# Two pieces for the first heads, four units per row of 256-column products, and a shorter halved tail in a float32 attention and feed-forward kernel

## The chip, the cores and the metric

One core of a Trainium2 chip runs one kernel. The metric is device time of an execution in microseconds (us); less is better. Three runs of the kernel before took 1053.59, 1054.35 and 1054.69 us, so its median is 1054.35 us.

## What is computed

Attention with a sigmoid in place of the softmax, then two feed-forward blocks on the 1792 tokens (4 batches of 448), all in float32:

```python
scores = scale * np.matmul(q, k.transpose(0, 1, 3, 2)) - np.log(S)
attn = 1.0 / (1.0 + np.exp(-scores))
x = np.matmul(attn, v)                       # 4 x 12 heads, 448 x 64, regrouped to 1792 x 768
h = x @ w_in;  r = np.maximum(h, 0.0);  g = s * (r * r) + b;   x = g @ w_out
h = x @ w_in2; g = np.maximum(h, 0.0) + alpha * np.minimum(h, 0.0);  y = g @ w_out2
```

Widths are 768 (model) and 2048 (inner). The feed-forward weights arrive as 64-bit floats.

## The kernel before, in words

**Attention.** 24 pairs of heads give 84 steps. Step u issues the score products of its 128 keys (`emit_qk`, four matmuls of 64x448), the sigmoid on ACT (`emit_sig`), and, two steps behind, the products with V (`emit_av`). Ahead of it, `NWARM` = 6 rounds of four matmuls on a tile of zeros (L345) keep the engine at work while the first DMA is under way. `load_kq(0)` fetches the first pair's q and k with two DMAs of SP's queue, 576 columns and then 320.

**Feed-forward.** The tokens go in groups: 768 tokens, 512 and 512 for the first block, and the same for the second. For each group there are 34 *units*: 16 of the first product (kind "in", six blocks of 128 rows each) and 18 of the second (kind "out": six outputs, each in three cuts of 6, 5 and 5 blocks). I number the units of a group 0 to 33. A float32 operand is split into a high part `hi` and a rest `lo`, and three products (hi by hi, hi by lo, lo by hi) are summed. For a group of 768 tokens, 512 of the columns take these three products (L411 to L413, 512 columns each, called *longs* here together with L416), and the other 256 tokens take one matmul of 512 columns that covers hi by hi and hi by lo at once (L416) and one of only 256 columns for lo by hi (`short`, L402, called *shorts*). A unit of six blocks thus has 24 longs and 6 shorts. Even units do the shorts last and odd units first, so that the shorts of two units stand in one row.

**The other engines.** The loop over `steps` sets the order on every engine. In step n it issues: the products of unit n; `evac` of unit n-1; `split_unit(n + 2)`; `fetch(n + 5)`. `split_unit` makes a unit's weights: `hi` by a cast on ACT (L99), `lo` by a subtraction on DVE (L102); without it no matmul of that unit that uses `lo` can run. `evac` of an "in" unit copies the sums on ACT (L437), then adds, squares and scales on DVE (L439, L447, L454; in the second block L461 and L465), casts on ACT (L210) and subtracts on DVE (L217): that makes `g`, the operand of the "out" units. `fetch` loads weights, or, where they still are 64-bit (for "out" units in the first use), converts them (`convert`: L141 on ACT, L147, L152 and L155 on DVE). Every engine works through its own list in order. PE's tiles of sums are four, the split weights have four buffers.

**The last unit** (L494) runs as two halves of 256 columns over its five blocks; the copy (L501) and the store of the first half overlap the second half; the add (L503) and a second store end the kernel.

Of the kernel before, what the change touches and what calls it, by code (L numbers as in the profile page):

```python
# [12 lines left out]
ALU = mybir.AluOpType  # L13
# [3 lines left out]
P = 128  # L17
OUT_CUTS = [(0, 6), (6, 11), (11, 16)]

PASSES = [(0, 0), (0, 1), (0, 2), (1, 0), (1, 1), (1, 2)]  # L20
N5 = 512
NWARM = 6

# [13 lines left out]
def tile_kernel(  # L37
# [13 lines left out]
    nc = tc.nc  # L51
    B, NPR, _, SKQ = kq.shape
    S = SKQ // 2
    NCH = vt.shape[4]
    D = vt.shape[5]
    NK = NPR
    DM = NK * P
    NFC = w_in1.shape[0]
# [5 lines left out]
    TG = N5 + REST  # L64
    TOK = [TG, N5, N5]
    TOK0 = [0, TG, TG + N5]
    NCUT = len(OUT_CUTS)
    PER = NFC + NK * NCUT
# [22 lines left out]
    def t_tile(name):  # L91
        return tp.tile([P, TG], F32, tag="t", name=name)
# [27 lines left out]
    uses = [m * PER + j for m, _ in PASSES for j in range(PER)]  # L120
    r64, w32, wraw, whl = {}, {}, {}, {}
# [76 lines left out]
    x, x_dram, xr = {}, {}, {}  # L198
# [41 lines left out]
    kqt, vtt, sct, sgt, avt = {}, {}, {}, {}, {}  # L240
# [7 lines left out]
    def buffer(what, cols):  # L248
        first, n = place[what]
        t = ga[first + taken[what] % n]  # L250
        taken[what] += 1
        return t[:, WMAX : WMAX + cols]

    def tiles(u):

        q, c = order[u]
        if c == NCH - 1:
            return [(h, q + h, c * P) for h in range(2)]
        return [(h, q, c * P + h * D) for h in range(2)]

    def load_kq(q):
        if q < B * NPR:
            bb, pr = divmod(q, NPR)
            kqt[q] = buffer("kq", SKQ)

            cuts = [0, S + P, SKQ] if q == 0 else [0, SKQ]
            for a, e in zip(cuts, cuts[1:]):
                nc.sync.dma_start(out=kqt[q][:, a:e], in_=kq[bb, pr, :, a:e])

    def load_v(q):  # L270
        if q < B * NPR:
# [3 lines left out]

    def emit_qk(u):
        sc = acc_tile("sc") if u != 2 else av_tile("sc")
        for h, q, k0 in tiles(u):
            for j in range(2):
                rows = slice(j * D, (j + 1) * D)  # L280
                nc.tensor.matmul(  # L281
                    sc[h * D : (h + 1) * D, j, :S],
                    kqt[q][rows, S + k0 : S + k0 + D],
                    kqt[q][rows, :S],
                    start=True, stop=True,
                )
        sct[u] = sc

    def emit_sig(u):
# [50 lines left out]
    wp = av_tile("wp")  # L340
    for _ in range(NWARM):
        for h in range(2):
            for j in range(2):
                rows = slice(j * D, (j + 1) * D)
                nc.tensor.matmul(  # L345
                    wp[h * D : (h + 1) * D, j, :P], idle[rows, :D], idle[rows],
                    start=True, stop=True,
# [16 lines left out]
    for u in range(NU + 2):  # L364
# [7 lines left out]
        if u >= 2:  # L372
            q, c = order[u - 2]
# [5 lines left out]
        if u in conv_step:  # L379
            k = conv_step[u]  # L380
            w = ga[k][:, :WMAX]
# [11 lines left out]

    g, hp, op_ = {}, {}, {}

    def products(dst, p, terms, first, last, short_first):

        n = len(terms) - 1

        def short(start, stop):  # L400
            for k, (hi, lo, mv) in enumerate(terms):
                nc.tensor.matmul(  # L402
                    dst[:, N5:TG], lo, mv[:, 2 * N5 : N5 + TG],
                    start=start and k == 0, stop=stop and k == n, skip_group_check=True,
                )

        if p == 0 and short_first:
            short(first, False)
        for k, (hi, lo, mv) in enumerate(terms):
            end = last and k == n  # L410
            nc.tensor.matmul(dst[:, :N5], hi, mv[:, N5 : 2 * N5], start=first and k == 0, stop=False)  # L411
            nc.tensor.matmul(dst[:, :N5], hi, mv[:, :N5], start=False, stop=False)  # L412
            nc.tensor.matmul(dst[:, :N5], lo, mv[:, N5 : 2 * N5], start=False, stop=end)  # L413
        if p == 0:
            for k, (hi, lo, mv) in enumerate(terms):
                nc.tensor.matmul(  # L416
                    dst[:, N5 : 2 * N5], hi, mv[:, 2 * N5 :],
                    start=first and not short_first and k == 0,
                    stop=last and short_first and k == n,
                    skip_group_check=True,  # L420
                )
            if not short_first:
                short(False, last)

    def in_mm(p, fc, i):
        hp[fc] = (acc_tile, av_tile)[fc % 2]("hps").rearrange("p b s -> p (b s)")
        w = whl.pop(i)
        terms = []
        for kc in range(NK):
            cols = slice(kc * P, (kc + 1) * P)  # L430
            terms.append((w[:, 0, cols], w[:, 1, cols], x[kc]))
        products(hp[fc], p, terms, True, True, i % 2 == 1)

    def take(h, p, name):

# [39 lines left out]
        g[fc] = g_tile(fc).bitcast(F32R)[:, : 2 * TG]  # L475
        split_to(g[fc], t, 0, "A" if p == 0 else "V")

    def out_mm(p, dc, cut, i):
        c0, c1 = OUT_CUTS[cut]
        if c0 == 0:  # L480
            op_[dc] = (acc_tile, av_tile)[dc % 2]("ops").rearrange("p b s -> p (b s)")
        w = whl.pop(i)
        if i == len(uses) - 1:


            M = N5 // 2
            t = t_tile("o")[:, :N5]
            o2 = (acc_tile, av_tile)[(dc + 1) % 2]("ops2").rearrange("p b s -> p (b s)")
            for h in range(2):
                to = op_[dc] if h == 0 else o2  # L490
                for fc in range(c0, c1):
                    cols = slice((fc - c0) * P, (fc - c0 + 1) * P)
                    for k, o in ((0, N5), (0, 0), (1, N5)):
                        nc.tensor.matmul(  # L494
                            to[:, :M], w[:, k, cols],
                            g[fc][:, o + h * M : o + (h + 1) * M],
                            start=h == 1 and fc == c0 and k == 0 and o == N5,
                            stop=fc == c1 - 1 and k == 1,
                        )
                if h == 0:  # L500
                    nc.scalar.copy(t, op_[dc][:, :N5])  # L501
                else:
                    nc.vector.tensor_tensor(  # L503
                        out=t[:, M:], in0=o2[:, :M], in1=t[:, M:], op=ALU.add
                    )
                c = TOK0[p] + h * M
                nc.sync.dma_start(
                    out=out[dc * P : (dc + 1) * P, c : c + M], in_=t[:, h * M : (h + 1) * M]
                )
            return  # L510
        terms = []
        for fc in range(c0, c1):
            cols = slice((fc - c0) * P, (fc - c0 + 1) * P)
            terms.append((w[:, 0, cols], w[:, 1, cols], g[fc]))
        products(op_[dc], p, terms, c0 == 0, c1 == NFC, i % 2 == 1)

    def out_evac(m, p, dc):
        t = take(op_.pop(dc), p, "o")
# [13 lines left out]
    def evac(st):  # L532
        kind, m, p, c, cut = st
        if kind == "in":
            in_evac(m, p, c)
        elif cut == NCUT - 1:
            out_evac(m, p, c)

    def fetch(i):

        if i >= len(uses) or i in wraw:
            return
        j = uses[i]
        if j in JUST and j not in w32:
            w = wraw_tile()
            convert(j, w, "A")
            next64()
            wraw[i] = w
        else:
            load32(i)  # L550

    steps = []
# [6 lines left out]

    ahead = {PER + 2 + 4 * k: PER + k for k in range(NFC)}  # L560

    n_split, n_fetch = 2, 5
    pend = None
    for n, st in enumerate(steps):
        kind, m, p, c, cut = st
        o, r = divmod(n, PER)
        flush_stores()
        store32()
        if kind == "in":
            in_mm(p, c, n)  # L570
        else:
            out_mm(p, c, cut, n)
        if pend is not None:
            evac(pend)
        pend = st
        while n_split <= n + 2:
            split_unit(n_split)
            fetch(n_fetch)
            n_split += 1
            n_fetch += 1  # L580
        if kind == "out" and o + 1 < len(PASSES):

            kc, odd = divmod(r - NFC - 3, 2)
            if 0 <= kc < NK:
                key = (*PASSES[o + 1], kc)
                if odd:
                    make_x(key)
                else:
                    load_xr(key)
        if n in ahead:  # L590
            convert(ahead[n], t_tile("cw"), "A")
            next64()
# [42 lines left out]
```

## Time and profile before

| | us |
|---|---|
| median of three runs | 1054.35 |
| the profiled execution, its own time | 1053.89 |
| its span, first to last instruction | 1052.1 |
| PE busy (share of the span) | 1047.9 (100%) |
| DVE busy | 594.8 (57%) |
| ACT busy | 448.5 (43%) |

The span is the time from the first to the last instruction; 1.8 us of the profiled execution lie around it. Matmuls are pipelined and their ends are modelled, so "busy" on PE says that it was never without work, not that it ran at its peak. The "chain" is the sequence of work that ended last, each piece released by the one before it.

### The profile page before, as it was taken

What the parts mean: (1) busy time and instruction counts of PE and PEld (TensorE: products, weight loads), DVE (VectorE), ACT (ScalarE), POOL (GpSimd) and SP (SyncE); (2) the same over time, 40 slices, a digit from 0 to 9 for tenths busy, and PEclk for the clock granted to TensorE, in tenths of its full rate; (3) what the DMA queues carried; (4) which work ended last, traced back from release to release, by engine and by line L of the source; (5) the groups of instructions that cost most, each with busy time, mean ns of one, the idle gap of its engine ahead of it and who ended that gap; (6) DMA issues with size and microseconds to landing.
All of it is one profiled execution on the core that took longest, in us unless ns stands there. A gap on an engine that the chain in (4) does not pass through costs nothing.

```text
span 1052.1 us, 14275 instructions
## 1 busy us (share of the span) xinstructions
PE 1047.9 (100%) x5631; PEld 818.3 (78%) x5631; DVE 594.8 (57%) x881; ACT 448.5 (43%) x625; POOL 0.2 (0%) x4
## 2 busy tenths in 40 slices
PE   9999999999999999999999999999999999999998
PEld 4333388888888888888888888888888888888887
DVE  4765456687643775447745366786616652266521
ACT  6777733444332554335534333443314432344321
POOL 0000000000000000000000000000000000000000
PEclk9999999999999999999999999999999999999999
DMA  7787660048762545764566512468523235323330
GB/s 276 274 268 248 244 249 1 27 140 262 250 225 93 195 138 203 270 207 136 183 220 207 187 61 60 120 187 291 201 93 105 89 122 170 130 90 98 116 117 31
DMA packets 62131, 173.17 MB, mean 165 GB/s; under 512 B 8048, under 2 KB 10736, under 8 KB 62064
## 3 DMA queue, kind: packets, MB, share of 16 engines
q1 hardware_dynamic: 62064, 172.27, 49.1%
q8 instruction: 44, 0.72, 0.3%
q14 instruction: 23, 0.19, 0.1%
HBM read 132.92 MB, written 39.32 MB: 164 GB/s over the span
## 4 chain that ended last, share of the span: by engine, by line
PE 100%; DVE 0%; issue 0%; DVEq 0%
PE hps L411 12%; PE hps L412 12%; PE hps L413 12%; PE ops L411 12%; PE ops L413 12%; PE ops L412 12%; PE sc L281 6%; PE av L307 6%; PE ops L416 4%; PE hps L416 4%; PE hps L402 2%; PE ops L402 2%; PE ops L494 0%; PE wp L345 0%; DVE o L503 0%
## 5 line engine op out<-in xcount | busy, mean ns | idle before, releaser
L102 DVE TENSOR_TENSOR whl<-wraw,whl 128x768 fp32r<-128x768 f32 (+1 forms) x188 | 167.8, 903 | 130.8 <-ACT whl L99 130.1
L411 PE MATMUL hps<-x,whl 128*128 128x512 f32 x576 | 224.4, 390 | 0.0
L412 PE MATMUL hps<-x,whl 128*128 128x512 f32 x576 | 224.3, 389 | 0.0
L413 PE MATMUL hps<-x,whl 128*128 128x512 f32 x576 | 224.1, 389 | 0.0
L411 PE MATMUL ops<-g,whl 128*128 128x512 f32 x571 | 222.4, 389 | 0.0
L412 PE MATMUL ops<-g,whl 128*128 128x512 f32 x571 | 222.3, 389 | 0.0
L413 PE MATMUL ops<-g,whl 128*128 128x512 f32 x571 | 222.1, 389 | 0.0
L99 ACT CAST whl<-wraw 128x768 fp32r<-128x768 f32 (+1 forms) x188 | 146.7, 792 | 40.8 <-PE ops L413 25.5
L411 PEld LDWEIGHTS hps<-x,whl 128*128 128x128 f32 x576 | 108.2, 188 | 22.7 <-issue 0.7
L413 PEld LDWEIGHTS hps<-x,whl 128*128 128x128 f32 x576 | 108.1, 188 | 22.6
L412 PEld LDWEIGHTS hps<-x,whl 128*128 128x128 f32 x576 | 108.2, 188 | 21.8
L413 PEld LDWEIGHTS ops<-g,whl 128*128 128x128 f32 x571 | 107.2, 188 | 22.4
L412 PEld LDWEIGHTS ops<-g,whl 128*128 128x128 f32 x571 | 107.2, 188 | 21.7
L411 PEld LDWEIGHTS ops<-g,whl 128*128 128x128 f32 x571 | 107.2, 188 | 21.7
L291 ACT ACTIVATE ga<-sc,bias_t 128x896 f32<-128x896 f32 x84 | 84.5, 1008 | 33.2 <-PE sc L281 31.5
L217 DVE TENSOR_TENSOR g<-t,g 128x512 fp32r<-128x512 f32 (+1 forms) x128 | 77.2, 624 | 31.8 <-ACT g L210 28.6
L437 ACT COPY o<-ops 128x512 f32<-128x512 f32 (+1 forms) x35 | 23.1, 661 | 149.0 <-PE ops L413 92.1
L281 PE MATMUL sc<-ga 64*64 64x448 f32 x672 | 78.3, 544 | 0.0
L307 PE MATMUL av<-ga,ga 64*64 64x448 f32 x672 | 77.1, 536 | 0.0
L147 DVE SCALAR_TENSOR_TENSOR cva<-r,cva 128x768 f32<-128x768 f32 (+1 forms) x68 | 61.7, 908 | 6.0 <-ACT cva L141 4.7
L210 ACT CAST g<-t 128x768 fp32r<-128x768 f32 x32 | 26.7, 836 | 85.8 <-DVE t L465 42.0
L217 DVE TENSOR_TENSOR x<-xr,x 128x512 fp32r<-128x512 f32 (+1 forms) x36 | 22.7, 645 | 59.0 <-ACT x L210 59.0
(53 smaller groups left out, 817.3 us busy)
## 6 DMA issues: line engine op xcount, KB each, us to landing
wraw<-w SPq DMA_DIRECT2D x104, 384.0 KB, 3.1
r<-in_w_in SPq DMA_DIRECT2D x32, 768.0 KB, 5.1
r<-in_w_out SPq DMA_DIRECT2D x24, 640.0 KB, 5.1
wraw<-w SPq DMA_DIRECT2D x48, 320.0 KB, 3.5
ga<-in_qk SPq DMA_DIRECT2D x23, 448.0 KB, 5.2
r<-in_w_out SPq DMA_DIRECT2D x12, 768.0 KB, 5.4
w<-wraw SPq DMA_DIRECT2D x24, 320.0 KB, 5.7
ga<-in_vt SPq DMA_DIRECT2D x24, 256.0 KB, 5.3
```

Source lines behind the costliest of these rows:

```text
L99: nc.scalar.copy(hi, src)
L102: nc.vector.tensor_tensor(out=lo, in0=src, in1=hi.bitcast(F32), op=ALU.subtract)
L147: nc.vector.scalar_tensor_tensor(out=a.bitcast(F32), in0=hi.bitcast(F32), scalar=2.0**-112, in1=a.bitcast(F32), op0=ALU.mult, op1=ALU.max,)
L217: nc.vector.tensor_tensor(out=lo[:, a - o : e - o], in0=src[:, a - c0 : e - c0], in1=hi[:, a - c0 : e - c0].bitcast(F32), op=ALU.subtract,)
L281: nc.tensor.matmul(sc[h * D : (h + 1) * D, j, :S], kqt[q][rows, S + k0 : S + k0 + D], kqt[q][rows, :S], start=True, stop=True,)
L291: nc.scalar.activation(sg, sct.pop(u)[:, :, :S], AF.Sigmoid, bias=bias_t[:, 0:1], scale=QKSCALE)
L307: nc.tensor.matmul(avt[q][j * D : (j + 1) * D, h, :S], vtt[q][keys, j, c, :], sg[keys, j, :], start=first, stop=last,)
L402: nc.tensor.matmul(dst[:, N5:TG], lo, mv[:, 2 * N5 : N5 + TG], start=start and k == 0, stop=stop and k == n, skip_group_check=True,)
L411: nc.tensor.matmul(dst[:, :N5], hi, mv[:, N5 : 2 * N5], start=first and k == 0, stop=False)
L412: nc.tensor.matmul(dst[:, :N5], hi, mv[:, :N5], start=False, stop=False)
L413: nc.tensor.matmul(dst[:, :N5], lo, mv[:, N5 : 2 * N5], start=False, stop=end)
L416: nc.tensor.matmul(dst[:, N5 : 2 * N5], hi, mv[:, 2 * N5 :], start=first and not short_first and k == 0, stop=last and short_first and k == n,
```

## The change

- **First heads.** The host lays q and k out as k[:128], q, k[128:]. The first pair's DMA is cut at column 352: the first key tile with half of q on SP's queue, the rest on ACT's queue. Unit 0 of the attention runs its products in two halves of 224 columns. `NWARM` is 5 instead of 6.
- **Group of 768 tokens, both blocks (p = 0).** Units go in rounds of four. Units 0 and 1 of a round do their longs, then the shorts of both; units 2 and 3 do the shorts of both and then their longs. So 24 shorts (22 or so in "out" units) stand in one row instead of 12. Units 32 and 33 stay as they were. `unit_of` takes a unit's split weights and its tile of sums when the first of its matmuls is issued.
- **Order of a step, p = 0 only.** `split_unit(n + 2)` now stands ahead of `evac` of unit n-1.
- **Last unit.** Its first three blocks run with 512 columns, only the last two in halves.

```diff
-NWARM = 6
+NWARM = 5
...
-            cuts = [0, S + P, SKQ] if q == 0 else [0, SKQ]
-            for a, e in zip(cuts, cuts[1:]):
-                nc.sync.dma_start(out=kqt[q][:, a:e], in_=kq[bb, pr, :, a:e])
+            cuts = [0, P + S // 2, SKQ] if q == 0 else [0, SKQ]
+            for a, e, eng in zip(cuts, cuts[1:], (nc.sync, nc.scalar)):
+                eng.dma_start(out=kqt[q][:, a:e], in_=kq[bb, pr, :, a:e])
...
+    def products(n):
+
+        p, r = steps[n][2], n % PER
+        if p > 0:
+            longs(unit_of(n), p, False)
+        elif r >= PER // 4 * 4:
+            odd = r % 2 == 1
+            for part in (odd, not odd):
+                if part:
+                    shorts(unit_of(n), odd)
+                else:
+                    longs(unit_of(n), p, odd)
+        elif r % 4 < 2:
+            longs(unit_of(n), p, False)
+            if r % 4 == 1:
+                shorts(unit_of(n - 1), False)
+                shorts(unit_of(n), False)
+        else:
+            if r % 4 == 2:
+                shorts(unit_of(n), True)
+                shorts(unit_of(n + 1), True)
+            longs(unit_of(n), p, True)
...
+        c2 = c1 - 2
+        for fc in range(c0, c2):
+            cols = slice((fc - c0) * P, (fc - c0 + 1) * P)
+            for k, o in ((0, N5), (0, 0), (1, N5)):
+                nc.tensor.matmul(
+                    op_[dc][:, :N5], w[:, k, cols], g[fc][:, o : o + N5],
+                    start=False, stop=False,
+                )
...
         for h in range(2):
             to = op_[dc] if h == 0 else o2
-                for fc in range(c0, c1):
+            for fc in range(c2, c1):
...
-        if pend is not None:
+        if n == len(uses) - 1:
+            last_mm(p, c, cut, n)
+        else:
+            products(n)
+        if p > 0 and pend is not None:
             evac(pend)
+        split_unit(n + 2)
+        if p == 0 and pend is not None:
+            evac(pend)
+        fetch(n + 5)
         pend = st
```

**The rows of matmuls on PE at units 18 and 19** (in the first group). `ops_2084` holds the sums that unit 18 completes, `whl_2124` (before) and `whl_2109` (after) are the split weights of unit 18, and `whl_2162` are those of unit 19 in both; L402 is the short of before, L424 that of the change; L413 and L409 are the longs that use `lo`. Before:

```order
L413 MATMUL ops_2084<-g15_2120,whl_2124 128x512
L416 MATMUL ops_2084<-g11_1908,whl_2124 128x512
...
L402 MATMUL ops_2084<-g14_2067,whl_2124 128x256
L402 MATMUL ops_2084<-g15_2120,whl_2124 128x256
L402 MATMUL ops_2213<-g0_1425,whl_2162 128x256
L402 MATMUL ops_2213<-g1_1468,whl_2162 128x256
```

After, with `whl_2016` and `whl_2062` for units 16 and 17:

```order
L424 MATMUL ops_2084<-g5_1650,whl_2016 128x256
L424 MATMUL ops_2084<-g6_1686,whl_2062 128x256
...
L424 MATMUL ops_2084<-g15_2117,whl_2109 128x256
L424 MATMUL ops_2180<-g0_1428,whl_2162 128x256
...
L424 MATMUL ops_2180<-g5_1650,whl_2162 128x256
L407 MATMUL ops_2084<-g11_1905,whl_2109 128x512
```

The first matmul with the weights of unit 19 stood behind all longs of unit 18; now it stands ahead of them.

**The list of DVE from unit 12's evacuation to unit 19's weights** (same group). L439 and L482 are the first DVE step of an evacuation, L217 its last, L147 and L155 the first and last of a conversion, L102 the split. Before, beginning at the evacuation of unit 12 (`t_1956`):

```order
L439 TENSOR_TENSOR t_1956<-hps_1872,t_1956 128x256
...
L217 TENSOR_TENSOR g12_1961<-t_1956,g12_1961 128x256
L102 TENSOR_TENSOR whl_1965<-ga15_108,whl_1965 128x768
...
L217 TENSOR_TENSOR g15_2120<-t_2115,g15_2120 128x256
L102 TENSOR_TENSOR whl_2124<-wraw_1968,whl_2124 128x640
L147 SCALAR_TENSOR_TENSOR cva_2128<-r64_2027,cva_2128 128x640
L152 TENSOR_SCALAR wraw_2127<-r64_2027 128x640
L155 SCALAR_TENSOR_TENSOR wraw_2127<-cva_2128,wraw_2127 128x640
L102 TENSOR_TENSOR whl_2162<-wraw_2021,whl_2162 128x768
```

After (`t_1959` is unit 12's):

```order
L102 TENSOR_TENSOR whl_1956<-ga15_108,whl_1956 128x768
L482 TENSOR_TENSOR t_1959<-hps_1872,t_1959 128x256
...
L217 TENSOR_TENSOR g12_1964<-t_1959,g12_1964 128x256
L147 SCALAR_TENSOR_TENSOR cva_1969<-r64_1868,cva_1969 128x640
...
L102 TENSOR_TENSOR whl_2109<-wraw_1968,whl_2109 128x640
L482 TENSOR_TENSOR t_2112<-hps_1985,t_2112 128x256
...
L155 SCALAR_TENSOR_TENSOR wraw_2121<-cva_2122,wraw_2121 128x640
L102 TENSOR_TENSOR whl_2162<-wraw_2028,whl_2162 128x768
```

Each split moved ahead of one evacuation, so unit 15's weights (`whl_1965`, now `whl_1956`) no longer lie between; all else between unit 12's evacuation and unit 19's weights is what it was: four evacuations, four conversions and the splits of units 16 to 19.

## Rows read from the trace of the kernel before

**Rows 1.** Stretch 195 to 245: length, busy per engine (instructions), PEclk, DMA share, GB/s.
```profile
195.00:245.00 50.00, 50.00 (x244) 42.31 (x243) 41.38 (x63) 21.82 (x29) 0.00 (x0) 1.00 0.40 120
```

**Rows 2.** The chain, units 1 and 2 of the first group: start, us, what.
```profile
138.51 0.23 PE hps L411
...
142.62 1.36 PE hps L416 x6
143.98 0.23 PE hps L411
...
148.06 1.36 PE hps L416 x6
```

**Rows 3.** The chain, the shorts of units 12/13, 16/17 and 18/19, first group.
```profile
211.12 1.43 PE hps L402 x12
...
235.80 1.31 PE ops L402 x11
...
246.21 1.31 PE ops L402 x11
```

**Rows 4.** The timeline of ACT: the copy of unit 10's sums.
```profile
199.53 0.80 ACT L437 COPY t<-hps 128x768 f32<-128x768 f32 x1 [1.54 <-PE hps L402]
```

**Rows 5.** The timeline of DVE, 195 to 262.
```profile
200.36 0.42 DVE L439 TENSOR_TENSOR t<-hps,t 128x256 f32<-128x256 f32 x1 [1.17 <-ACT t L437]
...
204.38 0.95 DVE L102 TENSOR_TENSOR whl<-ga,whl 128x768 fp32r<-128x768 f32 x1
205.25 0.95 DVE L147 SCALAR_TENSOR_TENSOR cva<-r,cva 128x768 f32<-128x768 f32 x1
...
207.59 0.42 DVE L439 TENSOR_TENSOR t<-hps,t 128x256 f32<-128x256 f32 x1
...
214.48 0.42 DVE L439 TENSOR_TENSOR t<-hps,t 128x256 f32<-128x256 f32 x1
...
242.08 0.95 DVE L102 TENSOR_TENSOR whl<-wraw,whl 128x768 fp32r<-128x768 f32 x1
```

**Rows 6.** The chain, the shorts of units 12/13 and 16/17, second block's first group.
```profile
669.70 1.43 PE hps L402 x12
...
694.38 1.31 PE ops L402 x11
```

**Rows 7.** The timeline of DVE there: unit 12's evacuation, unit 19's weights.
```profile
672.90 0.42 DVE L439 TENSOR_TENSOR t<-hps,t 128x256 f32<-128x256 f32 x1
...
700.09 0.95 DVE L102 TENSOR_TENSOR whl<-wraw,whl 128x768 fp32r<-128x768 f32 x1
```

**Rows 8.** The chain, 0 to 16.
```profile
1.05 2.84 PE wp L345 x48
3.88 3.50 PE sc L281 x24
...
8.13 0.75 PE sc L281 x8
```

**Rows 9.** The timeline, 0 to 14: first DMA issues, weight loads, first sigmoid.
```profile
0.73 0.85 SPq L268 DMA_DIRECT2D ga<-in_qk  x2
...
3.69 0.30 PEld L281 LDWEIGHTS sc<-ga 64*64 64x64 f32 x8 [0.21 <-DMA ga<-in_qk]
...
5.53 1.01 ACT L291 ACTIVATE ga<-sc,bias_t 128x896 f32<-128x896 f32 x1 [3.31 <-PE sc L281]
```

**Rows 10.** DMA issues, 0 to 12: queue, count, KB each, median us to landing.
```profile
ga<-in_qk SPq DMA_DIRECT2D x1, 288.0 KB, 2.9
ga<-in_qk SPq DMA_DIRECT2D x1, 160.0 KB, 2.9
```

**Rows 11.** The chain, the last unit.
```profile
1045.40 3.60 PE ops L494 x30
...
1049.08 0.42 DVE o L503
```

**Rows 12.** The timeline, its first half's copy.
```profile
1047.23 0.59 ACT L501 COPY o<-ops 128x512 f32<-128x512 f32 x1 [8.06 <-PE ops L494]
```

More of the change, by code (lines that the diff above doesn't have):

```diff
@@ L277, in emit_qk @@
         sc = acc_tile("sc") if u != 2 else av_tile("sc")
[L278 to L286, printed above, removed]
+        n = S // 2 if u == 0 else S
+        for a in range(0, S, n):
+            for h, q, k0 in tiles(u):
+                k1 = k0 if k0 < P else k0 + S
+                for j in range(2):
+                    rows = slice(j * D, (j + 1) * D)
+                    nc.tensor.matmul(
+                        sc[h * D : (h + 1) * D, j, a : a + n],
+                        kqt[q][rows, k1 : k1 + D],
+                        kqt[q][rows, P + a : P + a + n],
+                        start=True, stop=True,
+                    )
         sct[u] = sc
@@ L394, in tile_kernel, with longs @@
     g, hp, op_ = {}, {}, {}
-    def products(dst, p, terms, first, last, short_first):
+    def longs(unit, p, short_first):
+        dst, terms, first, last = unit
         n = len(terms) - 1
[L400 to L408, printed above, removed]
         for k, (hi, lo, mv) in enumerate(terms):
@@ L421, in products, with shorts @@
                 )
[L422 to L432, printed above, removed]
+    def shorts(unit, short_first):
+        dst, terms, first, last = unit
+        n = len(terms) - 1
+        for k, (hi, lo, mv) in enumerate(terms):
+            nc.tensor.matmul(
+                dst[:, N5:TG], lo, mv[:, 2 * N5 : N5 + TG],
+                start=first and short_first and k == 0,
+                stop=last and not short_first and k == n,
+                skip_group_check=True,
+            )
@@ new lines, in tile_kernel, with unit_of @@
+    mms = {}
+    def unit_of(n):
+        if n not in mms:
+            kind, _, _, c, cut = steps[n]
+            w = whl.pop(n)
+            if kind == "in":
+                c0, c1, mv = 0, NK, x
+                hp[c] = (acc_tile, av_tile)[c % 2]("hps").rearrange("p b s -> p (b s)")
+                to = hp[c]
+            else:
+                (c0, c1), mv = OUT_CUTS[cut], g
+                if c0 == 0:
+                    op_[c] = (acc_tile, av_tile)[c % 2]("ops").rearrange("p b s -> p (b s)")
+                to = op_[c]
+            terms = []
+            for k in range(c0, c1):
+                cols = slice((k - c0) * P, (k - c0 + 1) * P)
+                terms.append((w[:, 0, cols], w[:, 1, cols], mv[k]))
+            mms[n] = to, terms, c0 == 0, c1 == (NK if kind == "in" else NFC)
+        return mms[n]
@@ L476, in in_evac, with last_mm @@
         split_to(g[fc], t, 0, "A" if p == 0 else "V")
-    def out_mm(p, dc, cut, i):
+    def last_mm(p, dc, cut, i):
         c0, c1 = OUT_CUTS[cut]
-        if c0 == 0:
-            op_[dc] = (acc_tile, av_tile)[dc % 2]("ops").rearrange("p b s -> p (b s)")
         w = whl.pop(i)
[L483 to L490, printed above, removed]
-                for fc in range(c0, c1):
[L492 to L504, printed above, removed]
-                    )
-                c = TOK0[p] + h * M
-                nc.sync.dma_start(
-                    out=out[dc * P : (dc + 1) * P, c : c + M], in_=t[:, h * M : (h + 1) * M]
-                )
[L510 to L515, printed above, removed]
@@ new lines, in last_mm @@
+        c2 = c1 - 2
+        for fc in range(c0, c2):
+            cols = slice((fc - c0) * P, (fc - c0 + 1) * P)
+            for k, o in ((0, N5), (0, 0), (1, N5)):
+                nc.tensor.matmul(
+                    op_[dc][:, :N5], w[:, k, cols], g[fc][:, o : o + N5],
+                    start=False, stop=False,
+                )
+        M = N5 // 2
+        t = t_tile("o")[:, :N5]
+        o2 = (acc_tile, av_tile)[(dc + 1) % 2]("ops2").rearrange("p b s -> p (b s)")
+        for h in range(2):
+            to = op_[dc] if h == 0 else o2
+            for fc in range(c2, c1):
+                cols = slice((fc - c0) * P, (fc - c0 + 1) * P)
+                for k, o in ((0, N5), (0, 0), (1, N5)):
+                    nc.tensor.matmul(
+                        to[:, :M], w[:, k, cols],
+                        g[fc][:, o + h * M : o + (h + 1) * M],
+                        start=h == 1 and fc == c2 and k == 0 and o == N5,
+                        stop=fc == c1 - 1 and k == 1,
+                    )
+            if h == 0:
+                nc.scalar.copy(t, op_[dc][:, :N5])
+            else:
+                nc.vector.tensor_tensor(
+                    out=t[:, M:], in0=o2[:, :M], in1=t[:, M:], op=ALU.add
+                )
+            c = TOK0[p] + h * M
+            nc.sync.dma_start(
+                out=out[dc * P : (dc + 1) * P, c : c + M], in_=t[:, h * M : (h + 1) * M]
+            )
@@ L560, in tile_kernel @@
     ahead = {PER + 2 + 4 * k: PER + k for k in range(NFC)}
-    n_split, n_fetch = 2, 5
     pend = None
@@ L568, in tile_kernel @@
         store32()
-        if kind == "in":
-            in_mm(p, c, n)
-        else:
-            out_mm(p, c, cut, n)
-        if pend is not None:
+        if n == len(uses) - 1:
+            last_mm(p, c, cut, n)
+        else:
+            products(n)
+        if p > 0 and pend is not None:
             evac(pend)
+        split_unit(n + 2)
+        if p == 0 and pend is not None:
+            evac(pend)
+        fetch(n + 5)
         pend = st
[L576 to L580, printed above, removed]
         if kind == "out" and o + 1 < len(PASSES):
@@ L611 @@
     arrays = {
-        "qk": np.concatenate([q, k], axis=2).transpose(0, 1, 3, 2).reshape(B, H // 2, P, 2 * S),
+        "qk": np.concatenate([k[:, :, :P], q, k[:, :, P:]], axis=2).transpose(0, 1, 3, 2).reshape(B, H // 2, P, 2 * S),
         "vt": np.concatenate([v, v[:, :, S - P // 2 :]], axis=2)
```

## Prediction

> **What bounds the kernel now.** I read the stretches first: between 195 and 245 us PE is busy for all 50.00 us, DVE for 41.38, ACT for 21.82 [rows 1]. The reader is to see that PE sets the time and that DVE, in just this stretch, has little to spare: this is where "in" units are evacuated while "out" weights are converted. Then the chain, for the price of a unit: its 24 longs take 5.44 us, from 143.98 to 148.06 + 1.36, or 0.227 each [rows 2]; 12 shorts in a row take 1.43 and 30 matmuls of 256 columns at the end 3.60, so 0.12 each whatever the row's length [rows 3, 11]. PE has no gap there, so a change can gain only what its matmuls cost, and can lose whatever PE is made to wait. So, last, the timeline of DVE, for when the weights of a unit are ready.
>
> **The rows of shorts: what they save.** After a row of shorts the next 18 longs take 4.11 us (138.51 to 142.62) where they take 4.08 elsewhere (143.98 to 148.06) [rows 2]; its first short is 0.01 cheaper than the others (12 x 0.12 = 1.44 against 1.43). A row costs 0.02 net. A group of 768 tokens had 17 rows and gets 8 + 1 = 9; there are two such groups, so 16 rows fewer: 16 x 0.02 = **0.32 us less**. Ends: 0, if leaving a longer row costs more, and 0.48, if only the 0.03 counts.
>
> **The rows of shorts: what they bring forward.** In a round of four, the shorts of unit 2 and of unit 3 stand ahead of unit 2's longs. So unit 3's split weights are needed some 5 us sooner than before, and units 0 and 1 of the round end only after both have done their longs, so that their evacuations come late and close together. Both fall on DVE, which works through its list in order. The tight place is unit 19, the last of the round 16 to 19, in the first group:
>
> 1. Before, its weights were ready at 242.08 + 0.95 = 243.03 [rows 5] and first used after five shorts of the row at 246.21, at 246.81 [rows 3]: 3.8 us to spare.
> 2. When are they needed now? Unit 16's longs end at 235.80 as before [rows 3]. Unit 17's 20 longs follow (4.53), then 6 + 5 + 5 = 16 shorts of units 16, 17 and 18 (1.92): 242.25. The slack of 3.8 would shrink below zero even if DVE were not a bit later.
> 3. DVE is later. Unit 12 and 13 are the first two of a round. Unit 12's longs end at 211.12 [rows 3]; now unit 13's longs come next (5.44) and then unit 12's shorts (0.72): 217.28. Unit 10's copy began 0.03 after its last short (its row of shorts is one pair, 2 x 5.44 + 1.43 + 0.03 = 12.34, ahead of 211.12, so 198.78 + 0.72 = 199.50 against 199.53), took 0.80, and the add on DVE followed 0.03 later, at 200.36 [rows 4, 5]. So unit 12's add comes at 218.14. Before it came at 214.48 [rows 5].
> 4. Is DVE free by then? A round before, unit 8's add comes, by the same steps, at 186.44 + 5.44 + 0.72 + 0.86 = 193.46. From add to add DVE needs 4.89 with the next split (200.36 to 204.38, plus 0.87 to 205.25), and 2.34 more with a conversion (205.25 to 207.59) [rows 5]. Four evacuations and two conversions: 193.46 + 19.56 + 4.68 = 217.70. It waits 0.4 us for unit 12's data, so step 3 decides.
> 5. From unit 12's add to unit 19's weights DVE then does what it did before, back to back (214.48 to 243.03, 28.55 us) less one split (0.87), which now stands ahead: 27.68. Ready at 218.14 + 27.68 = 245.82. PE wants them at 242.25: it **waits 3.6 us**.
> 6. The second block's first group has the same rows: unit 12's longs end at 669.70, unit 16's at 694.38 [rows 6], unit 12's add was at 672.90, unit 19's weights ready at 701.04 [rows 7]. Now the add comes at 669.70 + 5.44 + 0.72 + 0.86 = 676.72, the weights at 676.72 + 28.14 - 0.87 = 703.99, and they are wanted at 694.38 + 6.45 = 700.83: it **waits 3.2 us**.
>
> Together **6.8 us more**. The move of a split ahead of an evacuation is counted in it: it is the 0.87; without it the waits would be longer. Bounds: each wait is a difference of two sums of some 30 us, whose rows repeat within 0.3 us, so 6.0 to 7.6. Behind the wait stand all longs of unit 18; nobody on ACT, DVE or SP waits for them soon. After unit 19 a step of DVE's list holds a split (0.87) and a conversion (2.34) [rows 5], with an add in one step of three and later the next group's operand in one of two: less than PE's time for a unit, so I count no further wait in a group. Tiles of sums are no new wait: the tile that unit 19 takes was last unit 13's, whose evacuation follows unit 12's by one step, over 10 us earlier. In rounds further back (units 0 to 11) conversions are absent and DVE has time. SP's loads for later conversions start later with them, but behind a PE that is later too.
>
> **The last unit.** 30 x 0.12 = 3.60 [rows 11] becomes 9 x 0.227 + 12 x 0.12 = 3.48: **0.12 less**. The second half now lasts 6 x 0.12 = 0.72, and the first half's copy, which starts 0.03 after that half (1045.40 + 1.80 = 1047.20 against 1047.23) and takes 0.59 [rows 12], still ends 0.1 before it; without that cover the add (0.42, [rows 11]) would start later by 0.1 at most.
>
> **The head.** One round of warming fewer frees PE 2.84 / 6 = 0.47 us sooner [rows 8]. But the first weight load waited for the DMA as it was (0.21 us) [rows 9], and a piece of 288 KB and one of 160 KB both took 2.9 us to land [rows 10]: the smaller first piece (176 KB) need not come sooner. I take **0**. For a gain: 0.47 us earlier, which counts half, since the first 24 score records take 3.50 us where 8 take 0.75 later (24 would take 2.25) [rows 8], that is TensorE starts at the lower of its two levels, 1.2 GHz, and rises to 2.4: -0.24. For a loss: the second piece was issued 0.43 later (two issues in 0.85 [rows 9]) and landed that much later; if both pieces now share the way, the first lands like the second did, 0.2 lost, and PE idles 0.47 us more while it should warm: +0.45 in all. ACT's table load now stands behind a DMA issue of some 0.43 us; its first sigmoid is at 5.53 [rows 9], long after. Splitting unit 0 into 224 columns moves no columns: 0.
>
> The Trainium skill speaks against this part: its page DMA: Bandwidth & Descriptors, section Issuing engines are not separate DMA queues, says that DMAs started from different engines run on the same 16 DMA engines and interleave. By that rule the first piece would land about when both have moved, and the head would be at the loss of 0.2 rather than at 0. No row here shows a DMA from ACT's queue beside one from SP's.
>
> **The sum.** 6.8 - 0.32 - 0.12 + 0 = +6.4 us. The profiled execution took 1053.89, which gives 1060.3; it lies 0.46 under the median of the three runs, 1054.35, so against the median I say **1060.7**.
>
> **Rivals.**
> - *DVE keeps ahead and PE never waits.* For it: PE had no wait at all before, and splits now come first in each step. Against it: steps 2 and 5, where the need moves 4.6 us forward and the supply 2.8 us back. It decides if unit 19's weights are ready by 242.25. Then only the gains are left: 1054.35 - 0.44 = 1053.9, which is no difference that can be measured (0.2%, 2.1 us, is about what a measurement tells from no change).
> - *TensorE's clock falls in the waits.* A PE without work for as long as these waits may go back to 1.2 GHz. The start has the price: from 1.05 PE worked some 5.3 us before its pace doubled (in 3.50 us, 24 records fit with 2.5 us at 0.187 each and the rest at half that) [rows 8], half of it lost: 2.6 us per wait, 1063.3 with one and 1066.0 with both. Against it: nothing in this trace shows a fall, since PE never stops. The Trainium skill's page TensorE: Matmul & The Clock Gate, section Why this matters for your kernels, warns that idle gaps between bursts of matmuls bring the lower clock back. No row here bears on it: the granted clock reads 1.00 in a stretch without a gap [rows 1].
> - *The rows save more than they cost:* a faster kernel by over 0.2% would need 2.1 us, and all gains at their ends make 0.48 + 0.12 + 0.24 = 0.84. Only a price that no row shows could do it.
>
> **Chances.** The waits as worked out, with the clock kept: 0.80. The clock falls as well: 0.10. No wait: 0.08. A gain over 0.2%: 0.02. Slower by over 0.2% is 0.90, within it 0.08, faster 0.02. The range takes the waits' bounds, the head's ends and a partial second wait below, and one fall of the clock above: 1058.0 to 1063.5; what it leaves out is no wait, both falls and a gain.
>
> **What would show it.** A wait of PE (L424, shorts) on DVE's L102 of some 3.6 us near 242 and 3.2 near 701, and none elsewhere; unit 12's add near 218.1; longs after it still at 0.23 us each (clock kept); the last unit 0.12 shorter; rows of 24 shorts in 2.87 us. Wrong would be: PE without idle time in both groups, or waits at other units.

## The result, and the profile after

The changed kernel took 1063.3 us (median of five runs, 1063.12 to 1066.36) beside 1054.38 of the kernel before (five runs, 1053.59 to 1054.93): a ratio of **1.0095, interval 1.0083 to 1.0106**. It is slower, as forecast, but by more than the 6.4 us that were forecast: by 8.9 between the medians, by 10.0 by the ratio. Taken on the 1054.35 of the prediction, the ratio gives 1064.4, outside its range. The profiled execution took 1063.78 us, 9.89 more than the one before.

The page of the changed kernel: busy time and instructions of each engine, then two lines of the span in 40 slices, and the chain's shares.

```profile
PE 1050.4 (99%) x5622; PEld 820.1 (77%) x5622; DVE 593.1 (56%) x881; ACT 446.6 (42%) x625; POOL 0.2 (0%) x4
...
PE   9999999998999999999999999989999999999998
...
PEclk9999999998999999999999999999999999999999
...
PE 94%; DVE 3%; issue 1%; ACT 1%; DMA 1%; ACTq 0%; DVEq 0%
```

PE, never without work before, now has an 8 in the tenth slice and one in the 27th, and in the tenth the clock that it was granted has an 8 as well. The second hole has no mark in the clock. The chain has DVE in it. The waits name the place (what waited, for what; us in total, times, the longest):

```profile
PE ops L424 <- DVE whl L102: 7.0, 2, 3.6
...
PE sc L286 <- DMA ga<-in_qk: 0.4, 1, 0.4
```

L424 is the short, L102 the split. PE's timeline shows both holes (start, us, what, in brackets the idle time ahead and who ended it), the first group in the first two rows, the second block's first group in the last two:

```profile
240.09 2.24 PE L424 MATMUL ops<-g,whl 128*128 128x256 f32 x16
245.97 1.62 PE L424 MATMUL ops<-g,whl 128*128 128x256 f32 x6 [3.63 <-DVE whl L102]
...
706.64 0.64 PE L424 MATMUL ops<-g,whl 128*128 128x256 f32 x4
710.66 0.59 PE L424 MATMUL ops<-g,whl 128*128 128x256 f32 x3 [3.39 <-DVE whl L102]
```

The 16 shorts of units 16, 17 and 18 are there, and unit 19's follow after the hole. The idle time in brackets counts from the modelled end of the short before. By starts the holes are larger: in the trace the 16th short starts at 241.95, so that the next could have started 0.12 later, at 242.07; it starts at 245.97, **3.90 us** later. In the second group the same sum gives 710.66 - (706.64 + 4 x 0.12) = **3.54**.

DVE's timeline of the changed kernel has what answers to [rows 5] and [rows 7]: unit 12's add, then the split of unit 19 in the first group and in the second:

```profile
218.14 0.42 DVE L482 TENSOR_TENSOR t<-hps,t 128x256 f32<-128x256 f32 x1 [0.70 <-ACT t L480]
...
244.13 0.83 DVE L155 SCALAR_TENSOR_TENSOR wraw<-cva,wraw 128x640 uint32<-128x640 uint32 x1
244.87 0.95 DVE L102 TENSOR_TENSOR whl<-wraw,whl 128x768 fp32r<-128x768 f32 x1
...
709.57 0.95 DVE L102 TENSOR_TENSOR whl<-wraw,whl 128x768 fp32r<-128x768 f32 x1
```

The windows around the first hole and over the second (length, busy per engine, then granted clock, DMA share, GB/s):

```profile
239.00:243.00 4.00, 3.33 (x22) 2.83 (x20) 2.98 (x6) 1.94 (x3) 0.00 (x0) 1.00 0.72 252
243.00:247.00 4.00, 1.03 (x5) 1.06 (x6) 3.86 (x6) 1.83 (x3) 0.00 (x0) 0.74 0.40 95
247.00:252.00 5.00, 5.00 (x15) 3.99 (x15) 4.18 (x7) 1.42 (x2) 0.00 (x0) 0.53 0.95 322
252.00:257.00 5.00, 5.00 (x24) 4.12 (x23) 2.35 (x5) 2.21 (x3) 0.00 (x0) 1.00 0.81 234
...
706.00:712.00 6.00, 2.61 (x20) 2.35 (x19) 5.23 (x8) 3.55 (x5) 0.00 (x0) 1.00 0.50 151
```

From 247 to 252 PE is busy all the time, at a mean granted clock of 0.53, and starts 15 matmuls where the next 5 us have 24. This is the lower of its two levels, 1.2 GHz for 2.4; the trace's record of the clock has it fall at 244.89, in the hole, and rise at 251.71. After the second hole it reads 1.00 throughout. The chain shows the other places of the change:

```profile
0.73 3.10 DMA ga<-in_qk
3.83 0.04 issue
3.87 3.49 PE sc L286 x32
...
142.52 2.87 PE hps L424 x24
...
1055.39 2.04 PE ops L530 x9
1057.43 1.44 PE ops L542 x12
```

PE's timeline shows the price of the fall: the first and the eleventh long behind unit 19's six shorts, in the first group and in the second:

```profile
247.39 0.63 PE L407 MATMUL ops<-g,whl 128*128 128x512 f32 x1
...
251.65 0.43 PE L408 MATMUL ops<-g,whl 128*128 128x512 f32 x1
...
711.45 0.40 PE L407 MATMUL ops<-g,whl 128*128 128x512 f32 x1
...
713.75 0.39 PE L408 MATMUL ops<-g,whl 128*128 128x512 f32 x1
```

At full pace six shorts and ten longs take 0.72 + 10 x 0.227 = 2.99 from the first start to the start of the next long. Behind the first hole they take 251.65 - 245.97 = 5.68, so the fall costs **2.69 us**. Behind the second, with the clock kept, they take 713.75 - 710.66 = 3.09, so that up to 0.1 of the 2.69 may belong to the hole.

**The sum.** From the first feed-forward product to PE's last, before took 917.65 us (131.34 to 1048.99 in its trace), the change 927.54 (131.32 to 1058.86), 9.89 more. The waits are 3.90 + 3.54, the fall is 2.69: 10.13. The remaining -0.24 is what the rows and the last unit save (0.44 by the forecast) less some 0.2 that is lost beside the holes: 0.1 behind the second one, as just shown, and 0.07 ahead of the first, where the 16th short starts 0.19 after the 15th instead of 0.12. In this profile the head left nothing: the feed-forward part began 0.02 earlier.

Four of the five runs have a mean granted clock of 0.997 and lie between 1063.12 and 1063.78. The fifth has 0.993 and took 1066.36, 3.1 more than the median, about what one more fall would cost. In which hole the clock fell in the runs without a profile is not recorded.

### The profile page after: what moved, and what is told of

The parts are those of the page before. It is cut to its first block, busy times and chain, and to the rows that moved or that the text cites. A ratio compares the mean times of both kernels' runs of the same rounds, so it can differ in the third digit from the quotient of the medians.

```text
span 1062.0 us, 14259 instructions
## 1 busy us (share of the span) xinstructions
PE 1050.4 (99%) x5622; PEld 820.1 (77%) x5622; DVE 593.1 (56%) x881; ACT 446.6 (42%) x625; POOL 0.2 (0%) x4
## 4 chain that ended last, share of the span: by engine, by line
PE 94%; DVE 3%; issue 1%; ACT 1%; DMA 1%; ACTq 0%; DVEq 0%
PE hps L407 12%; PE ops L407 12%; PE hps L408 12%; PE ops L408 12%; PE hps L409 12%; PE ops L409 12%; PE sc L286 6%; PE av L312 6%; PE ops L412 4%; PE hps L412 4%; PE ops L424 2%; PE hps L424 2%; ACT g L210 1%; DVE cva L147 0%; DVE whl L102 0%
## 5 line engine op out<-in xcount | busy, mean ns | idle before, releaser
L102 DVE TENSOR_TENSOR whl<-wraw,whl 128x768 fp32r<-128x768 f32 (+1 forms) x188 | 167.8, 902 | 139.6 <-ACT whl L99 138.8
L409 PE MATMUL hps<-x,whl 128*128 128x512 f32 x576 | 224.1, 389 | 0.0
L409 PE MATMUL ops<-g,whl 128*128 128x512 f32 x571 | 222.8, 390 | 0.0
L409 PEld LDWEIGHTS hps<-x,whl 128*128 128x128 f32 x576 | 108.1, 188 | 22.5
L409 PEld LDWEIGHTS ops<-g,whl 128*128 128x128 f32 x571 | 107.6, 189 | 22.5
L217 DVE TENSOR_TENSOR g<-t,g 128x512 fp32r<-128x512 f32 (+1 forms) x128 | 77.2, 624 | 31.8 <-ACT g L210 28.6
L286 PE MATMUL sc<-ga 64*64 64x448 f32 (+1 forms) x680 | 78.2, 539 | 0.4 <-DMA ga<-in_qk 0.4
L147 DVE SCALAR_TENSOR_TENSOR cva<-r,cva 128x768 f32<-128x768 f32 (+1 forms) x68 | 61.7, 908 | 5.7 <-ACT cva L141 4.3
L210 ACT CAST g<-t 128x768 fp32r<-128x768 f32 x32 | 26.7, 835 | 90.3 <-DVE t L508 44.3
L286 PEld LDWEIGHTS sc<-ga 64*64 64x64 f32 x680 | 24.7, 136 | 39.7 <-issue 32.8
```

What stands on the lines that cost most here:

```text
L147: nc.vector.scalar_tensor_tensor(out=a.bitcast(F32), in0=hi.bitcast(F32), scalar=2.0**-112, in1=a.bitcast(F32), op0=ALU.mult, op1=ALU.max,)
L217: nc.vector.tensor_tensor(out=lo[:, a - o : e - o], in0=src[:, a - c0 : e - c0], in1=hi[:, a - c0 : e - c0].bitcast(F32), op=ALU.subtract,)
L286: nc.tensor.matmul(sc[h * D : (h + 1) * D, j, a : a + n], kqt[q][rows, k1 : k1 + D], kqt[q][rows, P + a : P + a + n], start=True, stop=True,)
```

## Experiments

**Theories.** A: unit 19's shorts wait for weights that DVE's list delivers too late, and PE's clock falls in the first of the two holes (waits 7.4, clock 2.7, and 0.2 saved). B, a rival: the rounds of four cost by themselves (more tiles and weights held at once, a worse order), wherever they stand. C, another: the time went where the DMAs or the head wait, and DVE's lateness is hidden.

### Rounds of four only for the "in" units

```diff
-        elif r >= PER // 4 * 4:
+        elif r >= NFC:
```

> The change with the rounds of four kept for the 16 units of the first product only; the 18 units of the second stand in pairs as before. Theory (unit 19's weights are wanted too early; the longer rows as such cost nothing): no wait of PE near 242 or 705, the clock stays at 1.00, and only the gains are left, 8 rows fewer at 0.02 and 0.12 at the end: 1054.0 us, 0.3 under the kernel before, 9 under the change. Rival (the evacuations of units 12 and 13, late by the rounds, starve PE whatever the order at unit 19): a wait of 1 us or more stays at units 16 to 19, and the time is above 1057.

Measured: 1054.18 (ten runs) beside 1053.84 (19 runs), ratio 1.0004 [0.9995, 1.0013]. The trace has no wait of PE on L102, and the clock is 1.00. From the first feed-forward product to PE's last it takes 917.39 us, 0.26 less than before. So the whole loss behind the head comes from the rounds of the "out" units (16 and later), and rounds of four among "in" units do what they were worked out to do. B falls for these; for the "out" rounds the last two runs decide.

### The first hole filled

Between unit 18's shorts and unit 19's, 15 products of 512 columns go into unit 19's tile of sums, in both groups; the unit's own first product writes over them.

```diff
                 shorts(unit_of(n), True)
+                if r == NFC + 2:
+                    to, (hi, lo, mv) = unit_of(n + 1)[0], unit_of(n)[1][0]
+                    for _ in range(15):
+                        nc.tensor.matmul(
+                            to[:, :N5], hi, mv[:, N5 : 2 * N5],
+                            start=True, stop=True, skip_group_check=True,
+                        )
                 shorts(unit_of(n + 1), True)
```

> The change, with 15 more matmuls of 512 columns (3.4 us each time, their sums overwritten) between unit 18's and unit 19's shorts in both groups: PE works while it would wait. Theory (the wait costs its own 3.9 and 3.5 us, and the first one makes TensorE's clock fall, some 3 us more): the weights of unit 19 come no sooner, PE waits under 0.6 us each time, the granted clock is 1.000, and the time is 1060.2, about 3 under the change. Rival 1 (the clock fell for another reason, or its fall costs nothing of its own): 1063.3 as the change. Rival 2 (the wait is not one for a fixed moment, but follows what PE does): 6.8 us longer than the change, 1070.

Measured: 1061.08 (four runs, 1060.47 to 1062.45), ratio 1.0070 [1.0055, 1.0085]. Windows and PE's timeline of this kernel, to be held against those of the change:

```profile
247.00:252.00 5.00, 5.00 (x24) 4.14 (x23) 4.17 (x6) 2.49 (x4) 0.00 (x0) 1.00 1.03 320
```

```profile
239.56 2.25 PE L424 MATMUL ops<-g,whl 128*128 128x256 f32 x16
241.65 3.58 PE L477 MATMUL ops<-g,whl 128*128 128x512 f32 x15
245.35 0.85 PE L424 MATMUL ops<-g,whl 128*128 128x256 f32 x5
```

L477 are the added products. The last row is cut off by the end of the view. The weights are as late as ever: DVE ends unit 19's split at 245.29, which is 114.50 us after the first feed-forward product, as in the change (245.82 and 131.32). PE still waits for them, 0.28 us by starts, and the stretch after them runs 24 matmuls in 5 us at a clock of 1.00. From the first feed-forward product to the last the kernel takes 924.75 us (130.79 to 1055.54), **2.79 less** than the change. The two fills take 6.8 us and 0.3 of waiting is left, 0.3 less than the 7.44 of the holes, so at least 2.5 of this difference is the fall. By the ratios the difference is 1.0095 - 1.0070 = 0.0025, 2.6 us, by the medians 2.2. So the fall is worth 2.2 to 2.8 us here, beside the 2.69 read from the starts, and what remains of the loss is the wait itself. The time lies above the 1060.2 that were expected: the median by 0.9, the fastest of the four runs by 0.3, while the interval of the ratio (1059.6 to 1062.8) holds it.

### Unit 19's split one step earlier

```diff
-        split_unit(n + 2)
+        if not (p == 0 and r == NFC + 1):
+            split_unit(n + 2)
+        if p == 0 and r == NFC:
+            split_unit(n + 3)
```

> The change with unit 19's weights split one step earlier, ahead of unit 15's evacuation. Theory (DVE's list sets the wait): the weights are ready some 6 us sooner, before they are wanted; unit 15's operand comes one split (0.9) later, and a wait of 0.5 to 1.0 us is left at unit 18's last shorts; clock 1.00; 1055.3 us. Rival (the wait is for a tile of sums, a DMA or the conversion of these weights): the wait of 3.9 stays, 1063.

Measured: 1055.76 (ten runs), ratio 1.0019 [1.0009, 1.0028]; the clock stays at 1.00. The waits and the chain near the old hole:

```profile
PE ops L424 <- ACT g L210: 1.1, 2, 0.7
```

```profile
238.40 1.60 DVE whl L102 x2
240.00 0.34 DVE t L482
...
241.37 0.69 DVE t L497
...
242.08 0.84 ACT g L210
...
242.96 1.10 PE ops L424 x7
```

One split moved ahead of one evacuation and of one conversion takes the wait on L102 away, and both holes together shrink from 7.0 to 1.1 us in this view (by starts from 7.44 to 1.42). What is late next is unit 15's operand: two splits in a row (1.60) now stand ahead of its evacuation on DVE, and its cast on ACT (L210) ends just before unit 18's last short, the one that uses it, can run. This shows that DVE's order made the wait, and not a tile of sums, a DMA or the conversion of these weights. Neither gap brought the clock down. The 0.0019 is 2.0 us, of which 1.17 lie between the first feed-forward product and the last (918.82 against 917.65); the other 0.8 is about what the head costs alone (below).

### The evacuation ahead of the split, as before

```diff
-        if p > 0 and pend is not None:
+        if pend is not None:
             evac(pend)
         split_unit(n + 2)
-        if p == 0 and pend is not None:
-            evac(pend)
```

> The change with the order of a step as it was before: evacuation, then split. Theory (lists in order): ACT and DVE then meet the split of a round's unit 3 behind the evacuation of its unit 0, which cannot begin before the shorts at the end of unit 1; from there it takes 4.9 us to the split's end, and PE, which wants it after 0.7 us, waits over 4 us in each of the four rounds of the first product in both groups, and at unit 19: some ten waits, 40 us or more with the clock falling in some: above 1095. Rival (the order matters only at unit 19, by one split of 0.9): two waits of 4.8 and 4.4, 1065 to 1068.

Measured: 1106.41 (four runs), ratio 1.0500 [1.0483, 1.0518], mean clock 0.988. The waits:

```profile
PE hps L424 <- DVE whl L102: 35.4, 8, 4.5
PE ops L424 <- DVE whl L102: 2.2, 2, 1.1
```

Now the fourth unit of every round of "in" units waits: eight times, behind the shorts that start at 145.03, 176.00, 206.94 and 237.87, and four more in the second block. The two waits of 1.1 stand in the round of units 24 to 27 (behind 311.84 and 796.53); unit 19, where a wait was expected too, has none. DVE's timeline shows why the eight arise, in the first round, where no conversion is in its list yet:

```profile
144.74 0.43 DVE L482 TENSOR_TENSOR t<-hps,t 128x256 f32<-128x256 f32 x1 [10.26 <-ACT t L480]
145.20 0.96 DVE L490 SCALAR_TENSOR_TENSOR t<-t 128x768 f32<-128x768 f32 x1
146.20 0.68 DVE L497 TENSOR_SCALAR t<-t,s_t,b_t 128x768 f32<-128x768 f32 x1
147.82 1.03 DVE L217 TENSOR_TENSOR g<-t,g 128x512 fp32r<-128x512 f32 x2 [0.94 <-ACT g L210]
148.76 0.95 DVE L102 TENSOR_TENSOR whl<-ga,whl 128x768 fp32r<-128x768 f32 x1
```

DVE stands idle for 10.26 us, waiting for sums that come only at the end of a row, evacuates, and then splits the weights for which PE already waits. The new order of a step, which the prediction priced at 0.87 us in one place, is what keeps rounds of four from costing some 50 us. And the clock fell at each of the eight long waits, by the trace's record 0.04 to 0.74 us after PE had resumed, and stayed low for 3.41 us each time; at the two short ones it did not fall. The first:

```profile
151.00:154.00 3.00, 3.00 (x9) 2.32 (x8) 2.02 (x5) 1.56 (x2) 0.00 (x0) 0.51 0.02 5
154.00:160.00 6.00, 6.00 (x28) 4.96 (x27) 1.88 (x3) 0.80 (x1) 0.00 (x0) 1.00 0.00 0
```

The sum closes: by starts the eight long waits are 4.51 to 4.62 each and the two others 1.27, 39.2 together, and half of eight low stretches of 3.41 is 13.6: 52.8, where the part from the first feed-forward product to the last takes 969.96 - 917.65 = 52.3 more. A fall is cheaper here, 1.7 us, since the low stretch was shorter than in the change (244.89 to 251.71, 6.82).

### The head alone, from two queues and from one

The kernel before with the change's head (layout, cut at column 352, halves of 224, `NWARM` 5), and the same with both pieces on SP's queue:

```diff
-            for a, e, eng in zip(cuts, cuts[1:], (nc.sync, nc.scalar)):
+            for a, e, eng in zip(cuts, cuts[1:], (nc.sync, nc.sync)):
```

> The kernel before with the change's head alone: two pieces from two queues, unit 0 in halves, 5 rounds of warming. Theory (both pieces share the DMA engines and land together): the first piece lands at 3.8 to 4.0 us where it landed at 3.65, the first score product starts 0.2 to 0.35 later, which costs half of it while the clock is low: 0.1 to 0.2 over the kernel before, no difference that can be measured. Rival (the smaller piece comes sooner, and what else the trace showed was chance): it lands before 3.5, 0.1 to 0.2 faster.

> As the kernel with the head alone, but both pieces from SP's queue. Theory (it is the sharing that delays the first piece): alone on the queue the smaller first piece lands at 3.3 to 3.5, the second near 4.0; the first product starts 0.2 to 0.3 sooner than before; 0.1 faster than before, not measurable, but seen in the trace. Rival (the time to land does not hang on the other queue): the first piece lands at 3.8 or later here too.

Measured: two queues 1054.84 (11 runs), ratio 1.0010 [1.0001, 1.0019]; one queue 1053.92 (11 runs), ratio 1.0000 [0.9990, 1.0009]; before 1053.92 (33 runs). The DMA issues of the first 12 us, two queues (KB, us from issue to landing):

```profile
ga<-in_qk ACTq DMA_DIRECT2D x1, 272.0 KB, 3.6
ga<-in_qk SPq DMA_DIRECT2D x1, 176.0 KB, 3.4
```

and one queue:

```profile
ga<-in_qk SPq DMA_DIRECT2D x1, 272.0 KB, 2.8
ga<-in_qk SPq DMA_DIRECT2D x1, 176.0 KB, 2.4
```

From two queues the small first piece takes 3.4 us, longer than the 2.9 of the 288 KB that it replaces [rows 10]: both pieces were issued together and land almost together, at 4.16 and 4.35 us, later than the 3.8 to 4.0 that were expected. From one queue the first lands at 3.10, the second at 3.98, and the first score product starts at 3.23 instead of 4.21. With the second queue the head costs 0.9 us, 0.1% (interval 0.01 to 0.19%), more than the 0.1 to 0.2 us expected; the earlier start from one queue, though larger than expected, is worth nothing that these runs can tell. In the ten traces of this case the granted clock rose first at moments between 4.0 and 7.2 us; at half pace until then, a rise 1 us later costs some 0.5 us, about what a head can gain. It rose at 4.7 to 7.2 in the six traces of kernels with the second queue (mean 6.3), and at 4.0 to 6.2 in the other four (mean 5.1), which may be a part of the 0.9; so few traces do not show it.

### The change without the wait

Unit 19's shorts stand behind unit 18's longs again, in the first run with the head of before, in the second with the small first piece from one queue, halves and `NWARM` 5. All else is as in the change.

```diff
-            if r % 4 == 2:
+            if r == NFC + 2 or r == NFC + 3:
+                shorts(unit_of(n), True)
+            elif r % 4 == 2:
```

> The change without its head, and with unit 19's shorts moved behind unit 18's longs: one row of 16 and one of 6 where a row of 22 stood. Theory (only unit 19's early need cost time): no wait of PE, clock 1.00; from the first feed-forward product to the end 0.4 us less than before (917.65 there), 1053.5 to 1054 and not slower than before; whether it is faster lies within what five rounds can tell. Rival (the wait moves on to unit 20 to 23, or to unit 18): a wait of 0.5 us or more, 1055 or longer.

> As the kernel before this one, but with the smaller first piece, both pieces from SP's queue, unit 0 in halves and 5 rounds of warming: all that the traces so far count as a gain. Theory: 0.1 under the kernel before this one, 0.5 under the kernel before the change. Rival: no difference to the kernel before in either direction.

Measured: 1053.77 (11 runs), ratio 0.9999 [0.9991, 1.0008], and 1053.66 (11 runs), ratio 0.9998 [0.9989, 1.0007]. No wait of PE on L102 is left and the clock is 1.00. The windows and PE's timeline of the first of the two, where the change had its first hole:

```profile
239.00:243.00 4.00, 4.00 (x26) 3.55 (x25) 2.99 (x6) 2.16 (x3) 0.00 (x0) 1.00 0.69 242
243.00:247.00 4.00, 4.00 (x22) 3.36 (x21) 3.85 (x6) 1.62 (x3) 0.00 (x0) 1.00 0.45 108
```

```profile
239.86 2.25 PE L424 MATMUL ops<-g,whl 128*128 128x256 f32 x16
241.94 0.40 PE L407 MATMUL ops<-g,whl 128*128 128x512 f32 x1
```

From the first feed-forward product to the last the two take 917.47 and 917.43 us, 0.18 and 0.22 less than before, where 14 rows fewer at 0.02 and 0.12 at the end would give 0.40. Most of the rest lies in these two rows: the 16 shorts take 241.94 - 239.86 = 2.08 instead of 1.92, and 2.09 in the second kernel: the 16th, the only one that uses unit 15's operand, comes behind ACT's cast of it (L210, in the first kernel ending at 241.67, with the 16th short at 241.72). So a single row, unit 19's, carried the whole loss behind the head, and both B and C fall: the other rounds of the "out" units stand in these kernels, and their DMAs. Without that row and the second queue the change does nothing that can be measured, and no version here beats the kernel before.

## Why the prediction was right and wrong

- **What bounds the kernel; the place and the cause of the loss: right.** PE bounds it, a change can only lose what PE is made to wait, and the wait is that of unit 19's shorts on DVE's split, in both groups and at no other unit. The first run put the loss into the "out" rounds, the last two into this one row.
- **When the weights are ready (steps 3 to 5): right to the hundredth.** Unit 12's add was forecast at 218.14 and came at 218.14; the weights at 245.82, and they were ready at 244.87 + 0.95 = 245.82. Chaining DVE's list from measured durations held over 28 us.
- **The size of the waits (steps 2, 5 and 6): 0.3 short each.** 3.6 and 3.2 were forecast, 3.90 and 3.54 came. In the first, two small terms were left out: the first short starts 0.15 after the split ends (245.82 to 245.97), and PE was ready 0.18 sooner than forecast (242.07 for 242.25). Step 2 took 235.80 from the chain [rows 3], where a piece begins at the modelled end of the matmul ahead of it; by PE's timeline of before the shorts behind unit 16's longs started at 235.64. In the change unit 17's longs began at 235.56, and the 16 shorts took 242.07 - 240.09 = 1.98 for the 1.92 that were reckoned.
- **The rows and the last unit: right.** 24 shorts took 2.87 as forecast, the 18 longs behind them 4.11 (145.39 to 149.50 in the chain), the last unit 2.04 + 1.44 = 3.48. So 0.02 a row and 0.12 at the end came as forecast; of their 0.44 a net 0.24 is left in the sum, the rest being lost beside the holes.
- **The head: 0 was right for this profile, in part by luck, and its ground was not.** The first piece landed at 3.83, against 3.65 before, so the second queue did cost it the 0.2 that the prediction kept as an end; but the granted clock rose 0.23 earlier (5.95 for 6.18). Over eleven runs the same head alone cost 0.9 us (interval 0.1 to 2.0), twice the loss of 0.45 that the prediction kept as an end, though the interval holds both. The Trainium skill's page DMA: Bandwidth & Descriptors, section Issuing engines are not separate DMA queues, has that rule, that DMAs from several engines interleave on the same 16 DMA engines; the trace agrees: 3.83 and 4.01 us for the two pieces, and 3.10 and 3.98 with one queue.
- **The step that failed: "The waits as worked out, with the clock kept: 0.80. The clock falls as well: 0.10."** The clock fell in all five runs (mean granted clock 0.997 in four, 0.993 in the fifth, against 0.999 or 1.000 in the runs of the kernel before); in the profiled one it read 0.53 from 247 to 252 and cost 2.69 us. With the clock kept, the sum would have missed by the 0.6 of the waits and the 0.2 of the gains alone. The price was right: 2.6 us was worked out from the head of the kernel, and 2.69 by starts, 2.2 to 2.8 by the filled hole, were measured. That the rival's 1063.3 for one fall is the median to the tenth is luck, since its waits were 0.6 short. What was wrong is the weight. "Nothing in this trace shows a fall, since PE never stops" was put down as evidence against, when it is no evidence: a trace without a hole cannot show what a hole does. The Trainium skill's page TensorE: Matmul & The Clock Gate, section Why this matters for your kernels, warned that idle gaps between bursts of matmuls bring the lower clock back, and it was the only statement that bore on the question; the trace agrees with it for the first hole, and in the profiled run not for the second.
- **Range.** Its upper end took one fall with the waits at 6.8; with the waits at their own bound of 7.6 one fall already makes 1064.1. With the clock's fall at even odds the range would have had to reach to both falls, 1066.0, and would have held all runs but the 1066.36.

## What to carry to other kernels

Putting small matmuls of several units into one row saves 0.02 us a row, and asks for the weights of the last unit a whole unit's time earlier: before moving work forward on the engine that sets the time, chain the list of the engine that feeds it, from its measured durations, up to that need. Reckon for a hole of several us in a busy TensorE with its length and with a slow stretch that may follow, here 3.9 + 2.7 us for the first and 3.5 alone for the second; and do not take the absence of an effect in a trace that has no occasion for it as evidence against it. Where the supplier is late by so little, the cheap repair is to leave that one row where it was, or to bring one split forward and see what is late then (here that left a hole of 0.9 and one of 0.5 us).

## What the hardware showed that was not expected

- Holes of similar length fared differently: the first, 3.90 us, brought the lower clock; the second, 3.54 us, did not in the profiled run. Eight holes of 4.5 to 4.6 us all did; two of 1.3, and gaps of 0.9 us and less, did not. Why the second hole did not is open. The clock stayed low for 6.82 us in the change and for 3.41 each time in the run with eight falls, which cost 2.7 and 1.7 us.
- A DMA of 176 KB landed later when a second one started beside it from another queue (3.1 to 3.4 us in six traces) than when that one was issued behind it on its own queue (2.4 in two).
